# A gated scan laid out with (batch, head, segment) on the 128 rows: complex suffix scan step by step, one 96-deep product for W, head pairs in column tiles

## Chip, cores and metric

One core of one Trainium2 chip. The metric is the time on the device of one execution, in microseconds (us). Runs of a kernel have a state, fast or slow (over 1.5% above the fastest run of the same kernel); ratios and intervals use fast runs alone.

## The reference, cut to what matters

Batch 4, 8 heads, 768 time steps, head width 48; then 3072 tokens of width 384 go to one of 8 experts each (hidden width 1024).

```python
mag = np.sqrt(a_re * a_re + a_im * a_im)
scale = np.minimum(mag, 0.999) / (mag + 1e-06)
a_re_n, a_im_n = (a_re * scale, a_im * scale)
for t in range(S):                       # complex state S of D x D per head
    new_re = ar * S_re - ai * S_im       # ar, ai: row t of a, one value per state row
    new_im = ar * S_im + ai * S_re
    S_re, S_im = (new_re + kv, new_im)   # kv = outer product of k[t] and v[t]
    y[:, :, t] = q[t] @ S_re
# then: x = y as tokens; logits = x @ w_gate + modality_bias[modality_id]; one expert each
# out = gate * (relu(x @ w1[e]) @ w2[e])
```

A chunk of time steps can be done with matrix products if the cumulative product of the complex gates is known: with c[t] that product, W[s,t] = Re(sum over d of k[s]/c[s] times q[t]c[t]), masked to s <= t, and y = V W plus the old state times q c.

## The kernel before: the parts that matter

Chunks of 128 time steps, six of them, one after the other. The head width (48) lies on the rows, so every VectorE instruction of the scan has 48 of 128 rows and 4096 columns.

```python
L = 128
for c in range(NC):                                   # 6 chunks
    ...                                               # load, transpose (32 per tensor), copy
    nc.vector.reciprocal(tmp[:], tmp[:])              # 48 x 4096; the same again for k / |c|^2
    ...
    while d_ < L:                                     # log-step scan: 7 levels, 8 instructions each
        nc.vector.tensor_tensor(tA[:, :, :, :n_], a_hi, a_lo, Alu.mult)
        ...
        d_ *= 2
    ...
    for bh in range(BH):                              # 32 heads, one by one
        nc.tensor.matmul(Wt_ps[:], Kr[:], Qr[:], start=True, stop=False)      # 48-deep
        nc.tensor.matmul(Wt_ps[:], Ki[:], Qi[:], start=False, stop=True)      # 48-deep
        nc.vector.tensor_copy(Wt[:], Wt_ps[:])
        nc.gpsimd.affine_select(Wt[:], Wt[:], ...)                            # mask
        nc.tensor.matmul(y_ps[:], Wt[:], vb, start=True, stop=False)
        ...                                           # state products, transposes, state update
# then moe_sorted: routing, sort by expert, gathers, two products per tile of 128 tokens
```

## Time and profile before

| | before |
|---|---|
| time, median of 3 runs | 3883.63 us (3882.4 to 3884.83) |
| a chunk of 128 steps | 584 us, six of them to 3528 us |
| in it: scan / head loop | 239 us VectorE alone / 178 us |
| routing and loading of weights / experts | 80 us / 280 us |
| busy share PE, VectorE, ScalarE | 35%, 61%, 2% |

Every part of the span up to 3528 us belongs to the scan and the head loop. VectorE is full there about half of the time and TensorE waits for it; ScalarE does almost nothing. The rows and groups behind this are in the prediction below. In all profile lines PE is TensorE (one record is one pass; an f32 matmul takes two, a transpose one), PEld its loading of weights, DVE VectorE, ACT ScalarE and POOL GpSimd; `L84` is line 84 of that run's kernel, and `b<-a` means that b was written from a. PSUM is the memory that TensorE writes its products to. A tag is a name under which tiles take the same buffers in turn.

### The profile page before, as it was taken

Reading aid. Unit: us, or ns where it says so; the run is one execution under the profiler, and the core shown is the slowest. Engines: PE = TensorE matmul, PEld = TensorE weight load, DVE = VectorE, ACT = ScalarE, POOL = GpSimd, SP = SyncE. Lnnn points to the kernel's source line nnn. Section 1 sums busy time; section 2 is a strip of 40 time slices with the busy share of each in tenths; the row PEclk is TensorE's granted clock in tenths of the full one; section 3 lists DMA queues with packets and bytes.
Section 4 is the critical chain, followed back from the end, with each engine's and each line's share of the span. In section 5 each row is a group of like instructions: output and inputs, shape, how many; then the busy total and the mean of one; then the engine's idle time right before and its main releaser. Section 6 shows DMA issues by size and latency. Waiting matters only on the chain. (4 is left out here: it accounts for less than half of the span.)

```text
span 3888.1 us, 19678 instructions
## 1 busy us (share of the span) xinstructions
PE 1374.7 (35%) x5227; PEld 830.2 (21%) x5227; DVE 2385.9 (61%) x2837; ACT 64.6 (2%) x77; POOL 132.5 (3%) x281
## 2 busy tenths in 40 slices
PE   2002672002672002672002572002573001573898
PEld 0000450000450000450000451000451000451444
DVE  4997425997425997425997425998425998424111
ACT  0000000000000000000000000000000000000111
POOL 0000000000000000000000000000000000001221
PEclk9999999999999999999999999999999999999666
DMA  1000001000001000001000001000001000008210
GB/s 26 0 0 15 8 11 25 0 0 15 9 9 26 0 0 14 8 10 26 0 0 14 9 10 26 0 0 14 9 9 27 0 0 13 8 10 162 52 34 15
DMA packets 197622, 59.47 MB, mean 15 GB/s; under 512 B 171534, under 2 KB 192914, under 8 KB 197136
## 3 DMA queue, kind: packets, MB, share of 16 engines
q1 hardware_dynamic: 179552, 37.87, 4.8%
q0 software_dynamic: 17968, 20.36, 2.9%
q8 instruction: 50, 0.82, 0.1%
q14 instruction: 52, 0.43, 0.0%
HBM read 59.62 MB, written 15.53 MB: 19 GB/s over the span
## 5 line engine op out<-in xcount | busy, mean ns | idle before, releaser
L283 PE MATMUL tp<-ident,raw 128*48 128x128 f32 x768 | 285.6, 384 | 2057.3 <-DVE qc L284 1317.9
L283 PEld LDWEIGHTS tp<-ident,raw 128*48 128x48 f32 x768 | 88.4, 116 | 2253.2 <-DVE qc L284 1408.5
L380 DVE COPY y_sb<-y_ps 128x48 f32<-128x48 f32 x192 | 39.6, 207 | 409.7 <-PE y_ps L378 409.7
L370 PE MATMUL Wt_ps<-are,cr 48*128 48x128 f32 x384 | 152.3, 499 | 107.0 <-DVE cr L353 107.0
L376 PE MATMUL y_ps<-vc,Wt 128*128 128x48 f32 x384 | 127.4, 431 | 160.3 <-POOL Wt L374 160.3
L208 PE MATMUL h_ps<-xgT,w1s 128*128 128x128 bf16 x744 | 169.4, 250 | 19.0 <-DVE xgT L201 13.4
L374 POOL TENSOR_SCALAR_AFFINE_SELECT Wt<-Wt 128x128 f32<-128x128 f32 x192 | 56.1, 292 | 3445.8 <-DVE Wt L373 3445.8
L373 DVE COPY Wt<-Wt_ps 128x128 f32<-128x128 f32 x192 | 55.8, 291 | 189.4 <-PE Wt_ps L371 189.4
L303 DVE RECIPROCAL cr<-cr 48x4096 f32<-48x4096 f32 x6 | 154.5, 25745 | 0.2
L349 DVE RECIPROCAL qc<-qc 48x4096 f32<-48x4096 f32 x6 | 154.4, 25733 | 0.0
L376 PEld LDWEIGHTS y_ps<-vc,Wt 128*128 128x128 f32 x384 | 96.5, 313 | 216.8 <-POOL Wt L374 216.8
L284 DVE COPY aim<-tp 48x128 f32<-48x128 f32 x192 | 52.6, 282 | 135.8 <-PE tp L283 135.6
L377 PE MATMUL y_ps<-S0rA,are 48*128 48x48 f32 x384 | 126.9, 429 | 0.0
L370 PEld LDWEIGHTS Wt_ps<-are,cr 48*128 48x128 f32 x384 | 95.8, 308 | 125.7 <-DVE cr L353 108.8
L284 DVE COPY are<-tp 48x128 f32<-48x128 f32 x192 | 52.0, 280 | 115.1 <-PE tp L283 114.4
L371 PE MATMUL Wt_ps<-aim,ci 48*128 48x128 f32 x384 | 121.1, 417 | 0.0
L378 PE MATMUL y_ps<-S0iA,kc 48*128 48x48 f32 x384 | 119.7, 410 | 0.0
L385 DVE COPY yT_sb<-yT_ps 48x128 f32<-48x128 f32 x192 | 54.2, 282 | 96.5 <-PE yT_ps L383 96.5
L284 DVE COPY qc<-tp 48x128 f32<-48x128 f32 x192 | 49.9, 280 | 102.4 <-PE tp L283 102.2
L378 PEld LDWEIGHTS y_ps<-S0iA,kc 48*128 48x128 f32 x384 | 104.3, 330 | 0.0
L371 PEld LDWEIGHTS Wt_ps<-aim,ci 48*128 48x128 f32 x384 | 104.3, 330 | 0.0
L201 DVE COPY xgT<-xg_ps 128x384 bf16<-128x384 bf16 x31 | 11.1, 357 | 150.3 <-PE xg_ps L199 150.3
(153 smaller groups left out, 2886.2 us busy)
## 6 DMA issues: line engine op xcount, KB each, us to landing
w1s<-in_moe_w_dram POOLq DMA_DIRECT2D x8, 768.0 KB, 31.2
w2s<-in_moe_w_dram POOLq DMA_DIRECT2D x8, 768.0 KB
vc<-in_v_dram SPq DMA_DIRECT2D x24, 192.0 KB, 3.5
raw<-in_a_re_dram SPq DMA_DIRECT2D x192, 24.0 KB, 1.7
raw<-in_a_im_dram SPq DMA_DIRECT2D x192, 24.0 KB, 1.7
raw<-in_q_dram SPq DMA_DIRECT2D x192, 24.0 KB, 1.7
raw<-in_k_dram SPq DMA_DIRECT2D x192, 24.0 KB, 1.7
x_rows<-y_sb SPq DMA_DIRECT2D x192, 24.0 KB, 1.5
```

Of the source, the lines that this page charges most:

```text
L208: nc.tensor.matmul(h_ps[:, f, :], w1s[:, bass.ds(te, 1), k, ff * 128:(ff + 1) * 128], xgT[:, k, :], start=(k == 0), stop=(k == KD - 1))
L283: nc.tensor.transpose(tp[:], raw[:], ident[:L, :L])
L284: nc.vector.tensor_copy(dst[:, b_, h_, :], tp[:])
L303: nc.vector.reciprocal(tmp[:], tmp[:])
L349: nc.vector.reciprocal(qf[:], qf[:])
L370: nc.tensor.matmul(Wt_ps[:], Kr[:], Qr[:], start=True, stop=False)
L371: nc.tensor.matmul(Wt_ps[:], Ki[:], Qi[:], start=False, stop=True)
L373: nc.vector.tensor_copy(Wt[:], Wt_ps[:])
L374: nc.gpsimd.affine_select(Wt[:], Wt[:], pattern=[[1, L]], compare_op=Alu.is_ge, fill=0.0, base=0, channel_multiplier=-1)
L376: nc.tensor.matmul(y_ps[:], Wt[:], vb, start=True, stop=False)
L377: nc.tensor.matmul(y_ps[:], Qr[:], S0r[bh][:], start=False, stop=False)
L378: nc.tensor.matmul(y_ps[:], negQi[:], S0i[bh][:], start=False, stop=True)
```

## The change

Its intent: use all 128 rows and three engines. Rows hold (batch, head, segment), 128 per round, two rounds; a segment is 96 steps, eight segments make a sequence. The running product is made step by step from the end of a segment to its start (a suffix product), so an instruction has 128 rows and 96 or 192 columns. Square, Ln, Exp and the sign changes go to ScalarE. Real and imaginary parts lie beside each other (96 rows after the transpose), so W is one 96-deep product. Two heads share a PSUM tile in two column tiles of 64. The second round's elementwise part may run beside the first round's products. The routing works on 96 rows instead of 128, and takes its logits from the attention's own products.

The diff is long; its core, with cuts marked `...` (the whole of the loop over chunks and heads above is removed):

```diff
+    L = 96
+    def elem(r):                                   # one round: 128 rows
+        for c in range(L // T - 1, -1, -1):        # 12 chunks of T = 8 steps
+            sq = st.tile([P, 2, T, D], F32, name="sq")
+            nc.scalar.activation(sq[:], ab[:], Act.Square)
+            m = st.tile([P, T, D], F32, name="m", bufs=3)
+            nc.vector.tensor_tensor(m[:], sq[:, 0], sq[:, 1], Alu.add)
+            nc.scalar.activation(m[:], m[:], Act.Ln, scale=1.0 / (0.999 * 0.999))
+            nc.scalar.activation(m[:], m[:], Act.Exp, scale=-0.5)
...
+            for t in range(t0 + T - 1, t0 - 1, -1):
+                nc.vector.tensor_tensor(x[:], A[:, t + 1, ...], an[:, t - t0]..., Alu.mult)   # 192 columns
+                nc.vector.tensor_tensor(A[:, t], x[:, 0], x[:, 1], Alu.add)                   # 96 columns
+            sq = st.tile([P, T, 2, D], F32, name="sqe", tag="sq")
+            nc.scalar.activation(sq[:], e, Act.Square)
+            m = st.tile([P, T, D], F32, name="me", tag="m", bufs=3)
...
+            nc.scalar.activation(m[:], m[:], Act.Ln)
+            nc.scalar.activation(m[:], m[:], Act.Exp, scale=-1.0)
...
+            nc.tensor.transpose(tp[:, i, :], Qh[:, t4 + i]..., ident[:])        # tq
+            nc.scalar.copy(QT[:, :, t0 + t4:t0 + t4 + 4], ...)
+    def units(r):                                  # 16 units: 8 segments x 2 batches, 8 heads each
...
+            nc.tensor.matmul(wp[:, i, :], KT[:, h4 + i, :], QT[:, p, :], start=True, stop=True)   # W
+            nc.vector.tensor_tensor(KW[:, h4:h4 + 4, C:], wp[:], mask..., Alu.mult)
...
+            for i in range(2):
+                j = j2 + i
+                for u in range(2):
+                    nc.tensor.matmul(py[u * 64:(u + 1) * 64, i, :], V[...], KW[...], start=True, stop=(g == 0))
+                if g:
+                    for u in range(2):
+                        nc.tensor.matmul(py[u * 64:u * 64 + D, i, C:], Zs[...], QT[...], start=False, stop=True)
...
+    elem(0)
+    for r in range(NR):
+        units(r)
+        if r + 1 < NR:
+            elem(r + 1)
```

## The prediction

> **What bounds the kernel now.** I read the page's busy rows first, then the busy times by stretch, then the groups by form for durations, and last the timeline of one head and of the routing. The forty-slice rows:
>
> ```profile
> PE   2002672002672002672002572002573001573898
> DVE  4997425997425997425997425998425998424111
> PEclk9999999999999999999999999999999999999666
> ```
>
> The reader is to see six equal periods, in each of which VectorE is full while TensorE is idle and then half full while TensorE works, and a short tail in which TensorE alone is busy at a lower granted clock. By stretch (columns: length, then busy time and count of PE, weight loads, DVE, ACT, POOL, then clock, DMA share, GB/s):
>
> ```profile
> 584.00:1168.00 584.00, 181.12 (x672) 115.61 (x672) 386.34 (x444) 3.62 (x1) 9.35 (x32) 1.00 0.05 9
> 671.00:910.00 239.00, 8.60 (x23) 2.65 (x23) 222.04 (x95) 3.62 (x1) 0.00 (x0) 1.00 0.01 2
> 990.00:1168.00 178.00, 133.84 (x546) 101.05 (x546) 49.97 (x227) 0.00 (x0) 9.35 (x32) 1.00 0.04 9
> 3528.00:3608.00 80.00, 31.69 (x113) 15.36 (x113) 17.25 (x48) 5.09 (x8) 18.38 (x26) 0.81 1.15 221
> 3608.00:3888.00 280.00, 256.16 (x1082) 121.14 (x1082) 32.14 (x61) 36.54 (x62) 57.34 (x58) 0.62 0.13 28
> ```
>
> A period is 584 us: 239 us of scan on VectorE, 178 us of the head loop, the rest loads, transposes and more elementwise work. Six of them and the start make 3528 us; the experts take 80 us to route and load and 280 us to multiply. In the scan every VectorE instruction has 48 of 128 rows (groups by form, first 640 us; busy, mean ns):
>
> ```profile
> L303 DVE RECIPROCAL cr<-cr 48x4096 f32<-48x4096 f32 x1 | 25.7, 25745 | 0.0
> L297 DVE TENSOR_TENSOR cr<-are 48x4096 f32<-48x4096 f32 x2 | 8.8, 4417 | 0.1
> L300 ACT ACTIVATE cr<-cr 48x4096 f32<-48x4096 f32 x1 | 3.6, 3616 | 84.0 <-DVE cr L299 84.0
> L300 ACT ACT_TABLE_LOAD x1 | 1.3, 1283 | 0.8 <-PEq L440 0.8
> L370 PE MATMUL Wt_ps<-are,cr 48*128 48x128 f32 x64 | 25.4, 499 | 17.8 <-DVE cr L353 17.8
> L397 PE MATMUL Pr_ps<-vc,KrT 128*48 128x48 f32 x64 | 12.7, 298 | 6.3 <-DVE KrT L391 6.3
> ```
>
> An f32 matmul is two instructions (64 for 32 heads). The head loop is a serial chain, not a full engine: of 5.48 us a head, PE waits for a copy, a mask and the next copy (timeline; the bracket is the idle time before):
>
> ```profile
> 3420.48 0.29 DVE L373 COPY Wt<-Wt_ps 128x128 f32<-128x128 f32 x1 [1.02 <-PE Wt_ps L371]
> 3420.84 0.29 POOL L374 TENSOR_SCALAR_AFFINE_SELECT Wt<-Wt 128x128 f32<-128x128 f32 x1 [5.18 <-DVE Wt L373]
> 3421.18 0.66 PE L376 MATMUL y_ps<-vc,Wt 128*128 128x48 f32 x2 [0.81 <-POOL Wt L374]
> ```
>
> **What the Trainium skill says.** (1) "VectorE: DVE Perf Modes", Mode 1× (REGULAR): one result per cycle, at 0.96 GHz, with f32 among its cases. The trace agrees: (4417 - 357) / (4096 - 192) = 1.04 ns an element, so a two-input f32 operation takes 157 + 1.04 N ns, whatever its rows. (2) "ScalarE: Activation LUTs", What ACT_TABLE_LOAD costs: 186 ns + 0.833 N, and about 1283 ns for a table load plus about 1380 ns of drain at each switch of set. The 3616 ns and 1283 ns above agree; no run here shows the drain. Its Table sets section says one set holds both exp and ln; no run shows which set the program will get. (3) "SBUF — State Buffer", Door 1: lines of 16 bytes, and a penalty for an access that crosses to a new one. The routing agrees: a 192-element operation with a strided operand took 615 ns against 357. (4) "TensorEngine Tiling (Array Packing)", PSUM Bottleneck: tiling speeds TensorE, not the emptying of PSUM. I therefore count nothing for the two column tiles beyond fewer, wider copies.
>
> ```profile
> L153 DVE TENSOR_TENSOR slot<-off,rank_ps 128x192 f32<-128x192 f32 x1 | 0.6, 615 | 0.0
> L110 DVE TENSOR_TENSOR sh<-lg,mx 128x192 f32<-128x192 f32 x1 | 0.4, 357 | 0.0
> ```
>
> **The change, part by part.** Removed: all of the 3528 us, and in the experts' stage the read of the transposed activations and the logits' matmuls. Added: two rounds of an elementwise part (12 chunks of 8 time steps on 128 rows) and 16 units each (2 batches by 8 segments, 8 heads a unit).
>
> *Elementwise, per chunk on VectorE.* Four operations of 384 elements at 556 ns and three of 768 at 956 ns are 5.1 us. The eight steps are a chain of one 192-element product (357) and one 96-element sum (257, from the line above); dependent operations start some 30 ns after the one before ends (574.80 to 575.19 for a 0.35 us operation in the routing), so 0.67 us a step, 5.4 us. Sum 10.5 us, 252 us over 24 chunks: a floor.
> *On ScalarE:* two squares of 768 (0.83 us each), seven passes of 384 (0.51 each), two 512-wide evictions into a strided tile (0.6 each, more if point 3 bites): 6.4 us. If Ln and Exp come from different sets, up to four switches of 1.28 us add 5.1 us (10.6 with the skill's drain).
> *On the path.* The chain of a chunk is square, sum, Ln, Exp, Copy, two products, two copies, eight steps, square, sum, Ln, Exp, two products, transposes, eviction: about 20 us end to end with a hand-over of 0.1 us at each change of engine, before table loads. Neighbouring chunks can overlap, but the two squares share two buffers in turn, and in the head loop of before nothing ever ran ahead within a shared tag: PE idled 0.8 us at the mask with later transposes ready. So I expect the next chunk's square only after this chunk's steps. The period is then steps 5.4, both squares 1.7, sum 0.6, Ln, Exp and Copy of the next chunk 1.5, those of the back half 1.0, two exposed table loads 2.6, two products 1.5, two negating copies 1.0, evictions in between 1.2, hand-overs 1: 17.5, say 18 us. Round 0: 12 x 18 + 10 to start = 226 us.
>
> *Units.* TensorE per unit: spacing per f32 pass from the timeline is about 0.23 us with 128 stationary columns (two passes in 0.46) and 0.1 with 48 (two in 0.2); transposes take one pass at about 0.2. Eight K transposes 1.6; eight W at 2 x 0.2 = 3.2; four Z transposes 1.0; eight V products, 192 columns moving, 2.9; eight Z products 1.8; logits 0.7; bf16 transposes 0.5: 11.7 us. ScalarE has about 4 us of evictions and 1.5 of issues, VectorE 3.3: neither binds. The segments drain the pipeline: the small logits transpose shares the tag of the next segment's K transposes, so each segment of two units pays some 2 us at its head and 2 at its tail, (2 x 11.7 + 4) / 2 = 13.7 us a unit; with imperfect order 16. First segments lack Z. Each round about 250 us.
>
> *Overlap of rounds.* Round 1's elementwise part may start during round 0's units, since the running product is free then, but its transposed Q has one buffer and must wait for the last unit. I let the scans of six to seven of twelve chunks hide; visible: 15 us to finish those and 5.5 x 18 = 99, about 115 us.
>
> *Experts.* The multiply stage is unchanged: 280 us at the lower clock. The 80 us before it was 46 us to the logits, then the sort and the gathers; but POOL issues the weight loads before its iotas, the sort waited for those iotas (VectorE's `cand` waited 0.9 us for `pref` on POOL), and that stays. 64 instead of 48 matmuls to invert the permutation add 3.5 us; fewer bytes beside the weights take back about as much. 75 + 280 = 355 us.
>
> **Sum:** 226 + 250 + 115 + 250 + 355 + 4 = 1200 us.
>
> **The rivals.** *A: the elementwise part pipelines fully* and VectorE's 10.5 us, or ScalarE's 11.5 us with table loads, is the period. For: instructions of different tags did interleave before (transposed copies among the state updates at 588 us). Against: the shared tag above. 12 x 11.5 + 10 = 148, a visible round 1 of 80, units at 14: 148 + 220 + 80 + 220 + 355 = about 1025 us. *B: everything in a chunk is serial and each switch of set costs the skill's 2.66 us:* 20 + 4 x 1.5 to 2.66, say 28 us, so 346 + 260 + 200 + 250 + 355 = about 1410 us. For: the in-order head loop. *C: ScalarE binds the units*, through weightless waits of its DMA issues or slow strided evictions, and a unit takes 22 us: 226 + 350 + 115 + 350 + 355 = about 1400 us. Against: 5.5 us of work in 16. *D: the granted clock falls in the dense f32 units* as it does in the experts, from 1.00 to about 0.6: 11.7 becomes 19 us and a unit 22, again about 1400. Against: before, the head loop kept 1.00 while PE was 75% busy. *E: nothing gained*, a wait as long as the one removed: the units would have to take 90 us each, which no row suggests.
>
> **Range and chances.** Rivals A and B to D set the ends, 1025 and 1410; each has perhaps one chance in six, and they can mix. So 1030 to 1430. Even B and D together stay under 1800, so faster by over 2% has 0.98, within 2% 0.01, slower 0.01.
>
> **What would show each step.** VectorE's mean for the 192-element step near 357 ns, for the sum near 257; the busy rows with VectorE near 60% in round 0's first 226 us (10.5 of 18); 97 table loads if the sets differ, one or two if not; PE busy about 12 us a unit and 16 us between units; the clock 1.00 until the experts; the experts' multiply starting 75 us after the last unit and lasting 280. It is wrong if chunks are spaced under 13 or over 25 us, if units are spaced over 20, or if round 1's scan doesn't begin inside round 0's units.

## The result, and the profile after

The changed kernel took 1042.74 us (median of 4 runs, 1036.22 to 1047.4), beside 3883.31 us for the kernel before (4 runs, 3882.4 to 3884.83): ratio 0.2684, 95% interval 0.2666 to 0.2701. A ratio here is the mean time of one kernel's fast runs over that of the other's of the same rounds, so not quite the ratio of the medians quoted. The profiled one took 1047.4 us. The results are correct.

The forty slices (each about 26 us) of the kernel after:

```profile
PE   0101010139987787010129999940479999999997
DVE  3555555532555555646442243320511111111110
ACT  5566666632565667575732343320001111111111
PEclk9999999999876667555555698675556656666556
```

The six periods are gone. There are two bands in which TensorE is busy (units), two before them in which VectorE and ScalarE share the work at 50 to 70% each and neither is full (elementwise), and the experts at the end. By stretch, cut where the last transposed Q of a round and the last rows of a round were written (columns: length, busy time and count of PE, weight loads, DVE, ACT, POOL, then clock, DMA share, GB/s):

```profile
0.00:222.30 222.30, 22.95 (x96) 17.36 (x96) 119.39 (x282) 138.65 (x184) 1.35 (x10) 1.00 0.23 73
222.30:404.80 182.50, 152.23 (x1129) 113.73 (x1130) 83.61 (x189) 93.04 (x203) 3.23 (x16) 0.78 0.34 81
404.80:540.30 135.50, 20.45 (x96) 15.32 (x95) 76.49 (x173) 88.02 (x122) 0.00 (x0) 0.52 0.22 69
540.30:691.60 151.30, 137.41 (x1128) 104.37 (x1128) 46.19 (x84) 50.95 (x147) 2.63 (x13) 0.74 0.30 70
691.60:764.60 73.00, 15.02 (x69) 14.20 (x70) 20.08 (x47) 0.54 (x3) 17.41 (x25) 0.52 1.06 177
764.60:1045.70 281.10, 255.97 (x1082) 120.75 (x1082) 32.16 (x61) 36.54 (x62) 58.15 (x59) 0.62 0.09 28
```

| stage | predicted | measured | difference |
|---|---|---|---|
| elementwise, round 0 | 226 | 222.3 | -4 |
| units, round 0 | 250 | 182.5 | -67 |
| elementwise, round 1, visible | 115 | 135.5 | +20 |
| units, round 1 | 250 | 151.3 | -99 |
| routing, weights | 75 | 73.0 | -2 |
| experts | 280 | 281.1 | +1 |

So nearly all of the miss lies in the units. A chunk of the elementwise part came every 17.59 us. What it is made of (groups of the kernel after by form; busy, mean ns, then idle time before and what ended it):

```profile
L84 DVE TENSOR_TENSOR x<-A,an 128x192 f32<-128x192 f32 x192 | 68.6, 357 | 25.6 <-ACT an L81 19.9
L85 DVE TENSOR_TENSOR A<-x 128x96 f32<-128x96 f32 x192 | 49.4, 257 | 6.4
L72 ACT ACT_TABLE_LOAD x24 | 30.8, 1283 | 0.4
L93 ACT ACTIVATE sqe<-A 128x768 f32<-128x768 f32 x24 | 20.2, 843 | 95.2 <-DVE A L85 95.2
```

The two instructions of a step took 357 and 257 ns, as worked out. The same table-load line stands there for L73, L96 and L97: four loads a chunk, 97 in all with the first one (which is L68's). And ScalarE waited 95.2 us in all for the last step of a chunk (L85) before it could square it (L93). The order in which ScalarE then works (timeline of the kernel after; start, duration, and in brackets the idle time before):

```profile
71.98 0.84 ACT L93 ACTIVATE sqe<-A 128x768 f32<-128x768 f32 x1 [4.82 <-DVE A L85]
72.73 0.83 ACT L68 ACTIVATE sq<-ab 128x768 f32<-128x768 f32 x1
73.57 1.28 ACT L96 ACT_TABLE_LOAD   x1
74.87 0.52 ACT L96 ACTIVATE me<-me 128x384 f32<-128x384 f32 x1
75.41 1.28 ACT L97 ACT_TABLE_LOAD   x1
77.24 1.28 ACT L72 ACT_TABLE_LOAD   x1
```

`sq` of the next chunk comes right behind `sqe` of this one, though its input had long been there; then Ln, Exp, Ln, Exp, each behind a load of its own (the fourth, L73's, is not shown). This raised two theories for the 17.6 us: the shared tag holds the next square back (the prediction's step), and the four loads are all on the path (the prediction had only two there).

The units needed a closer look at the clock. Eight instructions of W (four heads; an f32 matmul is recorded as two) in the kernel after, first at 250 us, where the clock column says 1.00, then at 607 us, where it says 1.00 too (timeline, PE):

```profile
248.81 1.51 PE L139 MATMUL tk<-ident,KW 96*96 96x96 f32 x8
250.30 1.59 PE L145 MATMUL wp<-QT,KT 96*96 96x96 f32 x8
251.69 1.06 PE L150 MATMUL tz<-ident,Z 128*96 128x128 f32 x4
...
255.39 0.85 PE L160 MATMUL py<-KW,V 96*64 96x192 f32 x4
256.03 0.53 PE L164 MATMUL py<-QT,Zs 96*48 96x96 f32 x4
256.35 0.85 PE L160 MATMUL py<-KW,V 96*64 96x192 f32 x4
...
607.78 0.92 PE L145 MATMUL wp<-QT,KT 96*96 96x96 f32 x8
608.54 0.60 PE L150 MATMUL tz<-ident,Z 128*96 128x128 f32 x4
```

The same work took 1.39 us to the next start at 250 us and 0.76 us at 608 us. At 622.7 and 625.9 us, where the column says 0.50, it was 1.59 and 1.60 us long again, as at 250. So the first 1.00 is not a full clock: the column evidently holds 1.00 until the first change is recorded, and that comes only inside the first units. The Trainium skill, page "TensorE: Matmul & The Clock Gate", section Part 1: The HAM clock gate, says that half rate is the default and that only sustained work releases it. That agrees with the spacing here (1.39 against 0.76 us, a factor of 1.8). The trace of the kernel before shows the same of its own column (timeline, PE; the column says 1.00 at both lines, as everywhere before them):

```profile
3550.82 3.57 PE L100 MATMUL lgT_ps<-xT,wg 128*8 128x512 f32 x4 [43.95 <-DMA xT<-x_attn]
3554.55 1.88 PE L100 MATMUL lgT_ps<-xT,wg 128*8 128x512 f32 x4 [0.16 <-DMA xT<-x_attn]
```

Four equal instructions took 3.57 us and then 1.88, so the rate doubled there. No change is recorded before that, so as far as the record goes the whole attention of the kernel before ran at half rate, though its column said 1.00; and every duration from which I priced the units came from there.

### The profile page after: what moved, and what is told of

It reads as the page before. It is cut to its first block, busy times and chain, and to the rows that moved or that the text cites. A ratio compares the mean times of both kernels' runs of the same rounds, so it can differ in the third digit from the quotient of the medians.

```text
span 1045.7 us, 11696 instructions
## 1 busy us (share of the span) xinstructions
PE 604.0 (58%) x3599; PEld 385.7 (37%) x3599; DVE 377.9 (36%) x835; ACT 407.7 (39%) x716; POOL 82.8 (8%) x122
## 5 line engine op out<-in xcount | busy, mean ns | idle before, releaser
L106 PE MATMUL tq<-ident,Qh 128*96 128x128 f32 x192 | 43.5, 403 | 313.2 <-DVE Qh L100 310.0
L363 PEld LDWEIGHTS <-w1s 128*128 x744 | 76.4, 103 | 118.2 <-issue 42.6
L160 PE MATMUL py<-KW,V 96*64 96x192 f32 x512 | 88.4, 430 | 6.2 <-issue 4.6
L371 PE MATMUL y_ps<-w2s,hT 128*128 x248 | 83.7, 516 | 0.0
L145 PE MATMUL wp<-QT,KT 96*96 96x96 f32 x512 | 76.7, 319 | 3.9 <-ACT KT L140 3.9
L84 DVE TENSOR_TENSOR x<-A,an 128x192 f32<-128x192 f32 x192 | 68.6, 357 | 25.6 <-ACT an L81 19.9
L145 PEld LDWEIGHTS wp<-QT,KT 96*96 96x96 f32 x512 | 68.4, 226 | 14.1 <-ACT KT L140 7.4
L93 ACT ACTIVATE sqe<-A 128x768 f32<-128x768 f32 x24 | 20.2, 843 | 95.2 <-DVE A L85 95.2
L164 PE MATMUL py<-QT,Zs 96*48 96x96 f32 x448 | 51.8, 297 | 0.0
L85 DVE TENSOR_TENSOR A<-x 128x96 f32<-128x96 f32 x192 | 49.4, 257 | 6.4
L139 PE MATMUL tk<-ident,KW 96*96 96x96 f32 x256 | 44.1, 321 | 13.1 <-DMA KW<-kh 11.4
L173 PE MATMUL lg_ps<-yT,wgp 128*8 128x96 f32 x256 | 41.1, 299 | 10.7 <-ACT yT L170 9.7
```

The lines of the kernel that those rows point to most:

```text
L84: nc.vector.tensor_tensor(x[:], A[:, t + 1, :, None, :].broadcast_to([P, 2, 2, D]), an[:, t - t0].rearrange("p (u w) d -> p u w d", u=2), ...
L85: nc.vector.tensor_tensor(A[:, t], x[:, 0], x[:, 1], Alu.add)
L106: nc.tensor.transpose(tp[:, i, :], Qh[:, t4 + i].rearrange("p c d -> p (c d)"), ident[:])
L139: nc.tensor.transpose(tp[:, i, :], KW[:, h4 + i, 0:C], ident[:L, :L])
L145: nc.tensor.matmul(wp[:, i, :], KT[:, h4 + i, :], QT[:, p, :], start=True, stop=True)
L160: nc.tensor.matmul(py[u * 64:(u + 1) * 64, i, :], V[:, 2 * j + u, :], KW[:, 2 * j + u, :], start=True, stop=(g == 0))
```

## The experiments

Ten kernels ran, all correct, beside runs of the kernel before, whose medians were 3896 to 3897 us there: eight on one chip, e7 and e9 together on another. The kernel after again, unaltered, took 1038.11 us on the first (1030.3 to 1048.1, one of four slow), ratio 0.265; the others are to be compared with that.

> The changed kernel again, unaltered, as the control of this group on the same chip: 1030 to 1050 us; units of the first round 11.4 us apart, of the second 9.5; eight W passes in 1.59 us at the first units.

It gave the stages of the first trace within 7 us (units of round 0: first to last 159.4 us against 166.4; of round 1: 136.1 against 135.5). From the first units: eight instructions of W 1.48 and 1.6 us.

### Is the elementwise chunk bound by the shared buffers or by the table loads?

**e1_tags** gives the two squares and the two sums buffers of their own (the same bytes in all):

```diff
-            sq = st.tile([P, 2, T, D], F32, name="sq")
+            sq = st.tile([P, 2, T, D], F32, name="sq", bufs=1)
-            m = st.tile([P, T, D], F32, name="m", bufs=3)
+            m = st.tile([P, T, D], F32, name="m", bufs=2)
-            sq = st.tile([P, T, 2, D], F32, name="sqe", tag="sq")
+            sq = st.tile([P, T, 2, D], F32, name="sqe", bufs=1)
-            m = st.tile([P, T, D], F32, name="me", tag="m", bufs=3)
+            m = st.tile([P, T, D], F32, name="me", bufs=1)
```

> The two squares and the two sums of a chunk get a tag each, with the same memory in all (one buffer for each square, two and one for the sums). Theory (shared tags taken in turn are what holds the next chunk's square back until this chunk's steps are done): the next chunk's front half runs beside this chunk's steps, the period of a chunk falls from 17.6 us to ScalarE's own work, 6.4 + 4 table loads of 1.28 = 11.5 to 12.5 us, over the 19 chunks that aren't hidden behind units 95 to 115 us less, so about 935 us. Rival (the chain of hand-overs itself sets the period, the tags don't matter): period 17 to 18, within 10 us of 1043.

Measured: 951.26 us (949.84 to 958.93), ratio 0.2448 (0.2437 to 0.2458). The chunks came every 13.05 us. ScalarE's timeline in this run:

```profile
74.77 0.85 ACT L68 ACTIVATE sq<-ab 128x768 f32<-128x768 f32 x1 [0.26 <-DMA ab<-in_a_im_dram]
78.11 1.28 ACT L72 ACT_TABLE_LOAD   x1
...
82.22 0.83 ACT L93 ACTIVATE sqe<-A 128x768 f32<-128x768 f32 x1
```

Now the next chunk's `sq`, with its Ln and Exp and their loads, runs ahead of `sqe`, and `sqe` has no wait. The shared tag was a real gate, worth 4.5 us a chunk. (The edit parts the squares and the sums at once; which of the two held more was not tested.) It isn't the only one.

**e2_table** leaves the tags and loads one set once, ahead of everything:

```diff
+    nc.scalar.preload_act_table_set("natural_log_exp_and_others")
     identb = cpool.tile([128, 128], BF16, name="identb")
```

> The set that holds both Ln and Exp is loaded once at the start, so that no chunk loads a table. Theory (all four loads of a chunk lie on ScalarE's chain, none is hidden): one or two loads in the trace, the period 17.6 - 4 x 1.28 = 12.5 us, 19 x 5.1 = 97 us less: about 945 us. Rival (my prediction's sum, two exposed and two hidden behind VectorE): period about 15 us, 49 us less, 994. [...]

Measured: 916.7 us (905.84 to 925.19), ratio 0.2343 (0.2328 to 0.2358). The profiled run, 925.19 us, is slow; the chunk spacing quoted from it lies in a stage where TensorE is nearly idle. `sqe` starts in it:

```profile
79.07 0.84 ACT L93 ACTIVATE sqe<-A 128x768 f32<-128x768 f32 x1 [4.83 <-DVE A L85]
91.62 0.84 ACT L93 ACTIVATE sqe<-A 128x768 f32<-128x768 f32 x1 [4.83 <-DVE A L85]
```

12.55 us apart: 17.59 less four loads of 1.283 is 12.46. So all four loads of a chunk were on the path. The wait of 4.83 us for the steps is unchanged (the tag is still shared). The kernel gained more than the visible chunks: the units of round 0 shrank from 182 to 158.7 us (158.6 in e3 below, whose profiled run is fast). The chunks of round 1 that run behind them no longer put some twenty loads into ScalarE's queue among the units' copies, and TensorE's waits for ScalarE's copies of y (L170) fell from 9.1 to 2.6 us in all. That is only part of the 24 us; the clock column's mean rose too, from 0.78 to 0.87, and nothing here parts the two.

**e3_tags_table** does both.

> Both of the edits before. Theory: VectorE's own 10.5 us a chunk becomes the bound; period 10.5 to 11, 19 x 7 = 130 us less, about 910 us. Rival (the two gains add, 5.6 + 5.1): period below 8, which VectorE's work rules out; or (they share a cause) no better than the better of the two alone, about 935.

Measured: 844.62 us (841.69 to 858.8, one run slow), ratio 0.2167 (0.216 to 0.2174). Timeline, ScalarE, then VectorE:

```profile
93.68 0.84 ACT L93 ACTIVATE sqe<-A 128x768 f32<-128x768 f32 x1
102.93 0.84 ACT L93 ACTIVATE sqe<-A 128x768 f32<-128x768 f32 x1
```

```profile
93.96 0.55 DVE L76 SCALAR_TENSOR_TENSOR g<-m,g 128x384 f32<-128x384 f32 x1
94.43 0.25 DVE L85 TENSOR_TENSOR A<-x 128x96 f32<-128x96 f32 x1
94.60 0.95 DVE L79 TENSOR_TENSOR an<-ab,g 128x768 f32<-128x768 f32 x1
```

A chunk every 9.25 us. This is below the 10.5 us that the prediction called VectorE's floor. VectorE is the bound now, as the theory said (busy 8.90 of these 9.25 us), but the floor was put too high. It was a chain of dependent steps with 30 ns between them, plus all else behind it. Where nothing stands between them the steps do start 0.68 us apart (at 101.56 and 102.24 us); but elsewhere instructions of the neighbouring chunk fill the gaps, and an instruction that doesn't depend on the one before begins before that one ends: L76 begins at 93.96 and takes 0.55 us, L85 begins at 94.43. So durations that sum to 10.0 us (5.1 and 8 x 0.614) fit into 9.25. Alone the two gates are worth 87 and 121 us, together 194.

### Is it POOL's iotas, or the weights, that the experts wait for?

The prediction said that the sort waits for iotas behind 16 weight loads in POOL's queue, and that this stays in the 75 us. In the kernel after (waits of PE in that stretch: total, times, longest; and POOL's timeline):

```profile
PE rank_ps L278 <- DVE oneh L274: 39.4, 1, 39.4
PE xg_ps L354 <- DMA xg<-x_rows,idg: 3.4, 1, 3.4
```

```profile
728.01 0.90 POOL L222 DMA_DIRECT2D w2s<-in_moe_w_dram  x1 [3.12 <-DMA w2s<-in_moe_w_dram]
729.22 0.15 POOL L230 IOTA pref<- 96x8 f32 x1
760.46 1.04 POOL L350 DMA_INDIRECT xg<-x_rows,idg  x1 [30.74 <-DVE empty L344]
```

**e4_iota** moves the iotas and the masks ahead of the loads:

```diff
-    for e in range(E):          # 16 weight loads on gpsimd
-        nc.gpsimd.dma_start(out=w1s[:, e], ...)
-        nc.gpsimd.dma_start(out=w2s[:, e], ...)
     io128 = ...                 # iotas, masks, thr
+    for e in range(E):
+        nc.gpsimd.dma_start(out=w1s[:, e], ...)
+        nc.gpsimd.dma_start(out=w2s[:, e], ...)
```

> In the experts' stage the five small POOL instructions are placed before the 16 weight loads instead of after them. Theory (the sort waits 24 us for POOL, which is held by the issue of the weight loads, and this is on the path): cand starts 24 us sooner and so does the first expert matmul, about 1019 us. Rival (the gathers of the activations go through the same queue as the weight loads and land only when these are through, about 62 us after the loads began): the sort is early, but the first expert matmul is less than 10 us sooner, 1035 or more.

Measured: 1035.09 us (1031.3 to 1044.11), ratio 0.2657 (0.2641 to 0.2674), the same as the control's 0.265. The sort's `cand` came 6.6 us after the first load instead of 35.5, and the first gather was issued 39 us after it instead of 67. But the first expert matmul came 67.0 us after it, against 70.8: 27 us earlier at the gather, 4 us at the end. The timeline of that run:

```profile
728.03 1.04 POOL L351 DMA_INDIRECT xg<-x_rows,idg  x1 [3.38 <-DMA w1s<-in_moe_w_dram]
754.16 0.50 PE L355 MATMUL xg_ps<-identb,xg 128*128 128x128 bf16 x3 [28.12 <-DMA xg<-x_rows,idg]
```

The wait for the sort turned into a wait for the gather: issued at 728.0 (its indices were ready at 726.5), used at 754.2, behind the weights. The iotas' place was hidden by the weights; the number 75 was right, its cause wrong.

**e7_best** puts e1, e2 and e4 together; it is also the version that is to beat both kernels.

> The version that is to beat both kernels: separate buffers for the two squares and their sums, the table set with exp and ln loaded once, and POOL's iotas ahead of the weight loads. The first two together gave 844.6 us, the iotas alone 3.8 us at the start of the experts. If these add, about 840 us (825 to 845). Chunk period 9.2 us as with the first two; the experts' first matmul about 67 us after the last unit.

Measured: 837.96 us (831.99 to 847.04, five of six runs fast), ratio 0.215 (0.2142 to 0.2157). Beside e3's 0.2167 (on the other chip) the iotas add under 1%.

**e9_w1first** takes e7 and places the second weights after the first four gathers in the program:

```diff
     for e in range(E):
         nc.gpsimd.dma_start(out=w1s[:, e], ...)
-        nc.gpsimd.dma_start(out=w2s[:, e], ...)
...
+        if i == 0:              # the first four gathers, then the second weights
+            for n in range(4): ... nc.gpsimd.indirect_dma_start(out=xg[:], ...)
+            for e in range(E):
+                nc.gpsimd.dma_start(out=w2s[:, e], ...)
```

> As the version above, and the loads of the second weights are issued after the first four gathers, so that only the first weights are ahead of the gathers in POOL's queue. Theory: the time between units and experts is bound by the bytes ahead of the first gather (the first gather landed 26 us after its issue in the run with the iotas moved, and PE waited 28 us for it); half of the bytes ahead of it then make the first expert matmul come about 25 us sooner (40 to 45 us after the last unit, not 67), and the kernel 5 to 20 us faster, because the second product still needs all of the second weights. Rival: the sort is the bound: the first matmul moves by under 5 us and the time not at all.

Measured: 824.33 us (818.48 to 826.33), ratio 0.2113 (0.2107 to 0.2119): 1.7% faster than e7, the intervals apart. The first expert matmul came 54 us after the last unit, against 69. In e7 PE waited 28.1 us for the first gather. In e9 the wait of PE for it (total, times, longest), and from the timeline its issue:

```profile
PE xg_ps L365 <- DMA xg<-x_rows,idg: 12.9, 1, 12.9
```

```profile
526.55 1.03 POOL L353 DMA_INDIRECT xg<-x_rows,idg  x1 [18.18 <-DVE empty L344]
```

So bytes ahead of the gather did set its landing. The gain is 15 us and not the 25 expected. POOL sat 18.18 us idle until the sort's last product, so the gather could not be issued sooner; and it still took 13 us to land, since the edit did less than meant: four of the eight second loads were issued while POOL waited for the sort, so twelve of sixteen loads were still ahead of the gather.

### Why were the units cheaper than predicted?

After the result I held three things for possible: the two column tiles overlap (the prediction counted nothing for them), the units are a plain sum of TensorE's work with little around it, and the clock isn't what I thought.

**e5_cols** reorders the V and Z products, so that neighbours fall into the same column tile:

```diff
-    for i in range(2):
-        for u in range(2): V product (j2 + i, u)
-        for u in range(2): Z product (j2 + i, u)
+    for u in range(2):
+        for i in range(2):
+            V product (j2 + i, u)
+            Z product (j2 + i, u)
```

> The four V products (and Z products) of a PSUM tile are issued column tile by column tile, so that two consecutive matmuls fall in the same column tile and not in the other. Arithmetic, counts and waits stay. Theory: two column tiles run beside each other when their matmuls alternate (in the kernel after, passes of 192 columns follow each other in 0.16 us against 0.19 for W passes of 96 columns), and that is why a unit takes 9.5 to 11.4 us and not the 11.7 plus drains that I predicted. Then a unit gets 1.9 us longer at the full clock and 3.8 at the half: 60 to 120 us over 32 units. Rival: column tiles do nothing, the difference of passes is something else: within 10 us of the control. Between: 10 to 60 us, if TensorE's order is not the whole path of a unit.

Measured: 1060.85 us (1047.97 to 1065.47; the profiled run, 1065.47, is slow), ratio 0.2711 (0.2694 to 0.2728), some 2.3% above the control: between the two expectations. The edit does not end the alternation of column tiles, it halves it: a tile of PSUM takes eight V passes in the order 00 11 00 11 before and 00 00 11 11 after. The parts decide. In the first segment, where there are V products alone, at half clock, first in e5, then in the control:

```profile
577.65 1.55 PE L160 MATMUL py<-KW,V 96*64 96x192 f32 x8
```

```profile
555.18 1.55 PE L160 MATMUL py<-KW,V 96*64 96x192 f32 x8
```

The order changes nothing in the V products, and an overlap of neighbours in different tiles would have shown there even with half of the changes left. With Z products a group of eight instructions starts every 1.02 us in e5 and every 0.96 us in the control at half clock. Round 1's units, which have TensorE to themselves, took 138.4 us from the first to the last against 136.1 (at a mean clock of 0.82 against 0.77, so the spacings at one rate say more than these totals). The overlap theory predicted at least 30 us there and falls. The rest of the 22 us is, by the profiled run, in round 0 (168.9 against 159.4 us) and in some 13 us of round 1's chunks that no longer fitted behind it: another order of instructions gave another interleaving. What of that interleaving costs the time stays open; the run is slow, so these parts are rough. What a pass costs can be read from the lines of the kernel after at 255 us, all at half rate: a V pass (192 columns moving, 64 stationary) starts 0.16 us after the one before, a Z pass (96 and 48) 0.08, but a W pass (96 and 96) 0.17. V and Z go with their moving columns; W doesn't. Its load of weights is the suspect, and no run here varies it.

**e6_wtwice** does each W product twice into the same tile, with a mask of 0.5 so that the result is the same:

```diff
-    nc.vector.memset(mask[:], 1.0)
+    nc.vector.memset(mask[:], 0.5)
-    nc.tensor.matmul(wp[:, i, :], KT[...], QT[...], start=True, stop=True)
+    nc.tensor.matmul(wp[:, i, :], KT[...], QT[...], start=True, stop=False)
+    nc.tensor.matmul(wp[:, i, :], KT[...], QT[...], start=False, stop=True)
```

> Each W matmul is done twice into the same PSUM tile, and the mask holds 0.5, so the result is the same. Theory: units are bound by TensorE's passes, so that the added 16 passes a unit at 0.095 us (full clock) to 0.19 us (half) come out one for one: 1.5 to 3.0 us a unit, 49 to 96 us in all. Rival: a unit is a chain of hand-overs (transposes, copy, W, mask, copy) with slack on TensorE, and the additional passes fall into idle time: under 25 us.

Measured: 1062.14 us (1056.59 to 1074.87, one slow), ratio 0.2726 (0.2713 to 0.2738): 24 us more than the control by the medians, 30 by the ratios. That is at the edge of the rival's 25 and far under the theory's 49, so the total doesn't decide. In round 1, from first to last unit, the control and then e6:

```profile
549.30:685.40 136.10, 127.16 (x1067) 95.86 (x1066) 45.10 (x82) 47.78 (x136) 2.42 (x12) 0.77 0.28 65
```

```profile
555.10:701.10 146.00, 137.90 (x1305) 110.84 (x1304) 45.09 (x82) 47.17 (x135) 2.41 (x12) 0.86 0.27 62
```

The stretch grew by 9.9 us and PE's busy time by 10.7; the idle time stayed at 8 to 9 us. So these units are TensorE's work and little else, and the rival (additional work falls into idle time) is wrong there, whatever the total. My size was wrong for two reasons. A repeat costs a little less than a first product: a product and its repeat took 0.64 us at half rate and 0.34 at full in e6's timeline, one product in the control 0.35 to 0.38 and 0.19 to 0.21, so a repeat adds about 0.27 or 0.14 us, 2.1 or 1.1 us a unit. Over fifteen units that would still be 17 to 32 us. The other reason is in the two lines: the mean clock granted rose from 0.77 to 0.86. In this one trace denser work went with a higher rate; why is not settled here.

**e8_warm** gives TensorE work whose result nobody reads, in every chunk of round 0:

```diff
+            if r == 0:
+                dm = ps.tile([L, J, P], F32, name="dm", tag="xp")
+                for i in range(36):
+                    nc.tensor.matmul(dm[:, i % J, :], Qh[:, i % T]..., ident[:], start=True, stop=True)
```

> In each chunk of the first round 36 additional f32 matmuls of 128 columns (72 passes), whose result nobody reads, keep TensorE at work during the scan. Theory of a slow start: TensorE is at half rate at the first units because it idled before them; then eight W passes at the first units take 0.92 us in place of 1.59, a unit of round 0 about 7.5 to 9 us instead of 11.4, and the kernel is 40 to 60 us faster, less what the dummies cost the scan (0 to 10 us). Throttle theory: the rate is granted by how much work TensorE did recently; then the units of round 0 start no faster (1.59) or slow down further, and the time is the same or up to 40 us longer.

Measured: 1033.22 us (1025.81 to 1036.19), ratio 0.2645 (0.2634 to 0.2656), the same as the control's. Both theories have a part. The first units (timeline, PE) did run at full rate:

```profile
237.71 0.84 PE L149 MATMUL wp<-QT,KT 96*96 96x96 f32 x8
...
240.09 0.92 PE L149 MATMUL wp<-QT,KT 96*96 96x96 f32 x8
```

W in 0.84 and 0.92 us, where the control has 1.48 and 1.6; the second unit came 6.2 us after the first instead of 9.8. But from 246 us on the record shows 0.50, just after a stretch with gaps (windows of e8):

```profile
242.00:244.00 2.00, 1.26 (x14) 0.58 (x10) 1.08 (x2) 0.82 (x4) 0.20 (x1) 1.00 0.46 83
244.00:246.00 2.00, 1.05 (x10) 0.83 (x10) 1.78 (x3) 1.27 (x4) 0.00 (x0) 1.00 0.87 224
246.00:250.00 4.00, 3.99 (x21) 3.07 (x22) 0.55 (x1) 1.06 (x2) 0.00 (x0) 0.50 0.37 80
```

and at the end of the round e8 is 1.6 us ahead (its units had begun 3.7 us later). A warm start is taken back within a unit or two. How long the full rate takes to come back can be read in the kernel after (windows of round 1):

```profile
576.00:580.00 4.00, 4.00 (x25) 2.84 (x24) 0.35 (x1) 1.42 (x5) 0.12 (x1) 0.50 0.29 74
580.00:584.00 4.00, 4.00 (x37) 3.26 (x38) 1.11 (x2) 0.95 (x2) 0.00 (x0) 0.81 0.25 55
```

TensorE is busy without a gap from 568 us, and the rate returns after about 580. What exactly grants and takes it stays open; no run here varies that alone.

With this the units can be summed again, from the starts in the timelines above. At half rate: K transposes 1.49, two groups of W 1.39 + 1.52, Z transposes 0.99, V and Z products 1.19 + 3 x 0.96, logits and bf16 transposes 0.74 + 0.38 + 0.74 + 0.24: 11.6 us. At full rate the same items give about 6.3 us. PE's busy time was 152.23 / 16 = 9.5 us a unit in round 0 and 137.41 / 16 = 8.6 in round 1, at mean clocks of 0.78 and 0.74 (in round 0 the column's false 1.00 is in the mean); idle time around it was 1.9 and 0.9 us.

## Why the prediction was right or wrong, point by point

The time (1042.74 us) lies inside the range and at its lower end, 157 us below the number. The direction and its reason held: the scan left VectorE's 48 rows, and the 3528 us before the routing became 692.

- **Elementwise period, 18 us predicted, 17.6 measured.** Right in size, in part by luck, and half right in its reasons. The shared tag was a gate, as said (e1: 4.5 us a chunk). But the term "two exposed table loads 2.6" should have been four, 5.1 us (e2): the sum of 17.5 would then be 20.0, so other terms were too high by 2.4. The rest of the estimate of VectorE was right for single instructions (357 and 257 ns), and the "floor" of 10.5 us wrong: e3 ran at 9.25, with VectorE still the bound. (The times 574.80 and 575.19 that it gives stand in the trace at 3574.80 and 3575.19.)
- **Set for Ln and Exp.** The prediction left open whether the program would get the common set. It didn't: 97 loads. No drain is seen beside them: Ln started 0.01 to 0.02 us after a load's end.
- **Units, 16 us each predicted, 11.4 and 9.5 measured. This is the step that failed**, and it makes up -166 of the -157 us. The prediction put it as "11.7 us" of TensorE, "each segment of two units pays some 2 us at its head and 2 at its tail" for 13.7, and "with imperfect order 16". Two terms were wrong. The 11.7 is the cost at half rate (11.6) and was taken for the one at full rate; the kernel ran at a mix of the two, at 9.5 and 8.6. That a unit got full rate for part of its time was nowhere in the sum. And the 4.3 us for drains and order were 1.9 and 0.9: in round 1 PE waits 0.8 us between segments for the copy of the logits, not 4, and little else. In round 0 it also waits for ScalarE's copies of y (9.1 us in five times), so there the drains of 2 us a unit are about right in size, and only the 2.3 for "imperfect order" are missing. In round 0 the two are (11.7 - 9.5) x 16 = 35 and (4.3 - 1.9) x 16 = 38 us, in round 1 50 and 54. (The text rounded 16 x 16 to 250.)
- **Column tiles, nothing counted.** Right, against my own second thoughts: e5.
- **Overlap of the rounds.** Of twelve chunks five ran behind the units, not six to seven, and so 135.5 us were visible, not 115. That the transposed Q waits for the last unit held: its first copy of round 1 came at 406.0 us, 1.7 us after the last copy of round 0's units started.
- **Experts, 355 predicted, 354 measured.** Right in sum, because the stage was carried over from the trace before almost unchanged; wrong in cause (e4, e9). The sum is no sign that the cause was understood.
- **Clock "1.00 until the experts".** Wrong: from the first recorded change in round 0's units on it alternated between 0.50 and 1.00.
- **Rivals.** A (1025 us) came nearest in time, but for the wrong reason: the elementwise part did not pipeline, and the units were cheap. B's cost of a switch, 2.66 us, is refuted by e2 (1.28). C and D did not happen; D's mechanism, a lower clock, was there, but the durations I had started from held it already; the 1.00 that the prediction set against D was the false one.

## What to carry to other kernels

Before you price new work with durations from a trace, find out at which rate they were taken: compare the same instruction in two places, and do not rely on a clock column before its first recorded change. Buffers that two stages of a loop share in turn, and table loads between functions that one set could hold, were together worth 194 of 1038 us here, and both can be seen in one timeline of one period. When a wait is moved away and the end doesn't move, look at what the same engine waits for next: here it was the gather behind the weights, and ordering the bytes gained what ordering the instructions hadn't; the version with all of it took 0.2113 of the time of the kernel before, where the change alone took 0.265.

## What the Trainium skill lacked or had wrong

- "ScalarE: Activation LUTs", What ACT_TABLE_LOAD costs: it adds about 1380 ns of drain to each load. Here a switch cost the load alone: 1283 ns, Ln 0.01 to 0.02 us behind it, and 17.59 - 12.55 = 5.04 us for four.
- The same page, Table sets: its example counts one load for ln and then exp, as one set has both. That set exists and works, but unless it was loaded by name first the program got 97 loads, four for each of 24 chunks and one more.
- "TensorE: Matmul & The Clock Gate", Part 1: it gives some 3.4 us of sustained work to reach the full rate. In the kernel after, PE was busy without a gap from 568 us and the rate came back only after 580 us; and between 248 and 262 us it was busy 13.45 of 14 us with W still at half rate. The page's Part 4 says that transposes do not count as busy in the same way, and about a quarter of a unit's time at half rate (3.1 of 11.6 us) is transposes; whether that explains the delay no run here tests. The page warns that records of the clock can be unreliable, but not that a trace can show 1.00 before its first recorded change, while W takes 1.59 us in place of 0.92.
- "TensorEngine Tiling (Array Packing)": it has no figure for f32 products in two column tiles. Eight instructions of 192 columns took 1.55 us at half rate whether neighbours shared a column tile or not.
- "ScalarE: Activation LUTs", What ACT_TABLE_LOAD costs: the formula 186 + 0.833 N gives 612 ns for 512 elements. ScalarE's copies out of PSUM took less: 574 ns into a strided tile, 581 into a plain one. (The strided tile is no test of "SBUF — State Buffer", Door 1: its runs of four f32 values are 16 bytes, the line that the page gives.)
- No page that I read has the cost of a gather issued behind weight loads: 26 us from issue to use behind sixteen loads of 768 KB, about 13 us with four of them moved behind it.
